# Attention scores from high and low halves, and the keys' token mix moved to the receptance stage

## The chip, the cores and the metric

The kernel runs on one core of a Trainium2 chip. The metric is the device time in microseconds; three runs of the kernel before took 915.26, 916.33 and 917.14 us, so the median is 916.33 us. A difference under about 0.2% (1.8 us) can't be told from none here.

## The reference, cut to what matters

Four batches, 12 heads, 448 tokens, head size 64. Sigmoid attention feeds a two-layer gated mix over tokens and channels, and that feeds a mixer; only the parts that this case touches are shown in full.

```python
scores = scale * np.matmul(q, k.transpose(0, 1, 3, 2)) - np.log(S)
attn = 1.0 / (1.0 + np.exp(-scores))
x = np.matmul(attn, v)                      # heads side by side: (4, 448, 768)
xk = mu_k * x + (1.0 - mu_k) * x_prev       # x_prev: x one token later
xr = mu_r * x + (1.0 - mu_r) * x_prev
r = 1.0 / (1.0 + np.exp(-(xr @ w_r)))       # receptance
x = r * (np.maximum(xk @ w_k, 0.0) ** 2 @ w_v)
...                                         # mixer: w_tok1, w_tok2, w_ch1, w_ch2
```

## The kernel before, in words

The kernel works on two batches at a time, so everything happens twice. One round has three parts, written out one after the other in program order (the order on each engine is the order of the calls; nothing reorders it).

**Attention** takes 12 units. A unit is one batch and one pair of heads: the two heads lie in partitions 0 to 63 and 64 to 127 of a tile `heads[i % 3]`, which holds the keys, values and queries of that unit. `scores(i)` makes the scores in four chunks of 128 keys. For each chunk TensorE multiplies keys by queries, one matmul for each head, in plain float32, with 64 contraction rows each (L160); the two heads use the two row halves of the array. ScalarE turns a chunk into sigmoids (L169). `values(i)` multiplies the sigmoids by the values, again in float32, one head in each column half of the array (L176), and ScalarE copies the result to `xe` (L348), a tile of one pair of heads and both batches. After every second unit `mix` makes `xr` and `xk` of that pair on VectorE: four instructions each (L186 to L191), the last two of which split the mixed tile into a high half in float32r and the low remainder. Between these, in the first round only, ScalarE and VectorE prepare the first weights (`w_form` L195 and L196, `w_join` L199 and L202, `w_high` L240, `w_low` L244).

**First part**: six output tiles of receptance (`w_r` against `xr`), eight of `w_k` against `xk`, six of `w_v`, then the token mixer. Every product runs in `products` (L299) as three passes in float32r: high by high, high by low, low by high. Weights are prepared ahead of use in small steps that `tick` issues between products.

**Second part**: the channel mixer, whose last products also issue the loads of the next round's first two units.

SyncE issues all loads in one queue (`load_kq`, `load_v`, `w_raw`); a load waits there until its buffer is free.

Of the kernel before, what the change touches and what calls it, by code (L numbers as in the profile page):

```python
# [37 lines left out]
def kernel(  # L38
# [19 lines left out]
    def pool(name, bufs, **kw):  # L58
        return ctx.enter_context(tc.tile_pool(name=name, bufs=bufs, **kw))

    const = pool("const", 1)
    wraw, wpool, wsplit = pool("wraw", 3), pool("wpool", 3), pool("wsplit", 3)
    tmps = pool("tmps", 2)
    psum = pool("psum", 4, space=PSUM)

# [8 lines left out]
    two = const.tile([P, 2 * 4 * 2 * C], F32R, tag="two", name="two")  # L74
    three = const.tile([P, 4 * W], F32R, tag="three", name="three")
    rows = const.tile([P, NT, W], F32, tag="rows", name="rows")
    xes = [const.tile([P, 2, 1 + S], F32, tag="xe%d" % i, name="xe") for i in range(2)]

    def two_parts(t, kt):
        n = kt * W  # L80
# [17 lines left out]
    def beside(ap):  # L98
        return ap.rearrange("p (b n) -> p b n", b=2)

    heads = [const.tile([P, 2 * 4 * P + S], F32, tag="qkv%d" % i, name="qkv") for i in range(3)]
    kns = [t[:, : 4 * P] for t in heads]
    vns = [t[:, 4 * P : 8 * P].rearrange("p (h c d) -> p h c d", h=2, c=4) for t in heads]
    qns = [t[:, 8 * P :] for t in heads]

    def new_ps():
        return psum.tile([P, 1024], F32, tag="ps", name="ps")
# [12 lines left out]
    def load_v(i):  # L120
        b, pr = units[i]
        SP.dma_start(out=vns[i % 3], in_=v[b * NPAIR + pr])
# [29 lines left out]
    turn = [0]  # L152
    att = {}

    def scores(i):
        for c in range(4):
            ps = new_ps()
            for h in range(2):
                me = slice(h * D, h * D + D)
                PE.matmul(  # L160
                    ps[:, h * 512 : h * 512 + S],
                    kns[i % 3][me, c * P : (c + 1) * P],
                    qns[i % 3][me],
                    start=True,
                    stop=True,
                )
            a = beside(rows[:, turn[0] % NT])
            turn[0] += 1
            ACT.activation(a, banks(ps), AF.Sigmoid, bias=-math.log(S), scale=1.0 / math.sqrt(D))  # L169
            att[c] = a  # L170
# [10 lines left out]
    def mix(name, t, x, xe):  # L181
        m, om = mus[name]
        hi, lo = (p[:, t] for p in x)
        mixed = tmps.tile([P, W], F32, tag="tmp", name="mix")
        dst = beside(mixed)
        DVE.tensor_scalar(out=dst, in0=xe[:, :, 0:S], scalar1=om[:, t : t + 1], scalar2=None, op0=ALU.mult)  # L186
        DVE.scalar_tensor_tensor(
            out=dst, in0=xe[:, :, 1:], scalar=m[:, t : t + 1], in1=dst, op0=ALU.mult, op1=ALU.add
        )
        DVE.tensor_copy(hi, mixed)  # L190
        DVE.tensor_tensor(out=lo, in0=mixed, in1=f32(hi), op=ALU.subtract)  # L191
# [134 lines left out]
    def attention(b0):  # L326
        base = b0 * NPAIR
        for i in range(base, base + 2 * NPAIR):
            p, t, xe = i - base, (i - base) // 2, xes[(i - base) // 2 % 2]
            if i + 2 < base + 2 * NPAIR:  # L330
                load_kq(i + 2)
                if p:
                    load_v(i + 2)
            scores(i)
            if b0 == 0:
                if p < 3:
                    w_raw(p + 1)
                if p in (2, 4, 6, 8):
                    w_form(p // 2)
                    w_join(p // 2)  # L340
                if p in (3, 5, 7):
                    w_high((p - 1) // 2)
                    w_low((p - 1) // 2)
                    w_raw((p - 1) // 2 + 3)
            ps = values(i, xe)
            if p == 0 and i + 2 < base + 2 * NPAIR:
                load_v(i + 2)
            ACT.copy(xe[:, p % 2, 1:], ps[:, :S])  # L348
            if p % 2:
                mix("r", t, xr, xe)  # L350
                mix("k", t, xk, xe)

    def first_part(b0):
        if b0 == 0:
            tok2_load()
        for m in range(NT):
            w = weights()
            ps = new_ps()
            products(ps, WIDE, against(w, xr, NT))
            ACT.activation(rows[:, m], ps[:, :W], AF.Sigmoid)  # L360
            if b0 == 0 and m < 3:
                tok2_stage(m)

        for m in range(F // P):
            w = weights()
            ps = new_ps()
            products(ps, WIDE, against(w, xk, NT))
            hi, lo = kk(m)
            t = tmps.tile([P, W], F32, tag="tmp", name="sq")
            ACT.activation(t, ps[:, :W], AF.Relu)  # L370
            DVE.tensor_tensor(out=t, in0=t, in1=t, op=ALU.mult)
            ACT.copy(hi, t)
            DVE.tensor_tensor(out=lo, in0=t, in1=f32(hi), op=ALU.subtract)

        for m in range(NT):
            ps = new_ps()
            for part in range(2):
                w = weights()
                parts = [(w[0][:, t], w[1][:, t], *kk(4 * part + t)) for t in range(4)]
                hooks = {2: lambda: y_transpose(m - 1)} if m and part == 0 else {}  # L380
                products(ps, WIDE, parts, 4 * part, 8, hooks)
            DVE.tensor_tensor(out=rows[:, m], in0=rows[:, m], in1=ps[:, :W], op=ALU.mult)  # L382

        wt1 = [weights()]
        held = due[:]
        due.clear()
        for f in held:
            f()
        i = use[0]
        use[0] += 1  # L390
        wt1.append(halves.pop(i))
        for piece in range(3):
            ps = new_ps()
            ms = slice(2 * piece, 2 * piece + 2)
            for j in range(2):
                wh, wl = wt1[j]
                x = [t[:, :, ms].rearrange("p r m b c -> p r (m b c)") for t in y]
                parts = [(wh[:, r], wl[:, r], x[0][:, r], x[1][:, r] if r < 3 else None) for r in range(4)]
                products(ps[:, j * 512 : (j + 1) * 512], ((0, 512),), parts)
                if piece == 0 and j == 0:  # L400
                    y_transpose(NT - 1)
            hi, lo = (t[:, :, ms].rearrange("p j m b c -> p j (m b c)") for t in h1)
            psv = ps.rearrange("p (j n) -> p j n", j=2)
            ACT.activation(hi, psv, AF.Relu)
            DVE.scalar_tensor_tensor(out=lo, in0=psv, scalar=0.0, in1=f32(hi), op0=ALU.max, op1=ALU.subtract)
        due[:] = ahead(i)

        for m in range(NT):
            ps = new_ps()
            for b in range(2):  # L410
                parts = [(h1[0][:, j, m, b], h1[1][:, j, m, b], wt2h[:, j], wt2l[:, j]) for j in range(2)]
                products(ps[:, b * 512 : b * 512 + S], ((0, S),), parts)
            hi, lo = (beside(p[:, m]) for p in u)
            r = beside(rows[:, m])
            DVE.tensor_tensor(out=r, in0=r, in1=banks(ps), op=ALU.add)  # L415
            ACT.copy(hi, r)  # L416
            DVE.tensor_tensor(out=lo, in0=r, in1=f32(hi), op=ALU.subtract)  # L417

    def second_part(b0):
        for half in range(2):  # L420
            for f in range(6):
                w = weights()
                ps = new_ps()
                products(ps, WIDE, against(w, u, NT))
                hi, lo = (p[:, f] for p in h2)
                ACT.activation(hi, ps[:, :W], AF.Relu)  # L426
                DVE.scalar_tensor_tensor(  # L427
                    out=lo, in0=ps[:, :W], scalar=0.0, in1=f32(hi), op0=ALU.max, op1=ALU.subtract
                )
            for m in range(NT):  # L430
                w = weights()
                ps = new_ps()
                products(ps, WIDE, against(w, h2, 6))
                DVE.tensor_tensor(out=rows[:, m], in0=rows[:, m], in1=ps[:, :W], op=ALU.add)  # L434
                if half:
                    for b in range(2):
                        SP.dma_start(
                            out=out[b0 + b, m * P : (m + 1) * P], in_=rows[:, m, b * S : (b + 1) * S]
                        )
                    if m == 3 and b0 + 2 < B:  # L440
                        for i in range(2):
                            load_kq((b0 + 2) * NPAIR + i)
                            load_v((b0 + 2) * NPAIR + i)

    for b0 in range(0, B, 2):
        attention(b0)
# [4 lines left out]
def lay_out(x):  # L451
# [3 lines left out]
    def chunks(w, parts=1):  # L455
# [9 lines left out]
    tail = v[:, :, 3 * P :].transpose(0, 2, 1, 3)[:, :, :, None]  # L465
    y = {
        "q": qt,
        "k": np.concatenate([kt, kt[:, :, 3 * P :]], axis=2),
        "v": np.concatenate([head, np.concatenate([tail, np.zeros_like(tail)], axis=1)], axis=3),
        "moe_mu_k": x["moe_mu_k"].reshape(NT, P).T,  # L470
        "moe_mu_r": x["moe_mu_r"].reshape(NT, P).T,
        "moe_w_k": chunks(x["moe_w_k"]),
# [51 lines left out]
```

## Time and profile before

| | us |
|---|---|
| median of the runs | 916.33 |
| profiled execution, whole | 914.43 |
| its span on the core | 912.7 |
| TensorE busy | 900.8 (99%) |
| VectorE busy | 505.3 (55%) |
| ScalarE busy | 420.0 (46%) |
| scores, matmuls L160, busy | 78.9 |
| values, matmuls L176, busy | 77.4 |

The span is one execution from its first to its last instruction on the core; the 1.7 us between it and the execution's own time lie around it. TensorE is busy nearly all the time, so a share of time tells little: what counts is how long each stretch of matmuls takes. The two attention stretches run from 5.85 to 82.22 us and from 457.0 to 533.4 us. A matmul's duration in the profile reaches from its start to its modelled end, and several are in the array at once; the distance from one start to the next tells what one costs.

### The profile page before, as it was taken

The numbers are of one execution on the slowest core, as the hardware profiler recorded it, in microseconds if no ns is written. First come the engines' busy times: TensorE is split into PE (matmuls) and PEld (weight loads), VectorE is DVE, ScalarE is ACT, GpSimd is POOL, SyncE is SP. The second block draws the span as 40 slices with busy tenths as digits, with TensorE's granted clock in tenths as the row PEclk, the third lists the DMA queues.
The fourth block names the chain that finished last, engine by engine and source line by source line (L and its number), as shares of the span: only waits on it lengthen the run. The fifth ranks groups of instructions, "written<-read, shape, count | busy, mean of one in ns | idle before, by whom it ended". The sixth has DMA issues, their size and how long they took to land.

```text
span 912.7 us, 10954 instructions
## 1 busy us (share of the span) xinstructions
PE 900.8 (99%) x4464; PEld 723.8 (79%) x4464; DVE 505.3 (55%) x563; ACT 420.0 (46%) x550; POOL 1.2 (0%) x9
## 2 busy tenths in 40 slices
PE   9999999999999999999999999999999999999997
PEld 3335888888887888888843468888988878888886
DVE  1776546656657555555535564465566575555551
ACT  5784645544434443343355644455444354334420
POOL 0000000000000000000000000000000000000000
PEclk9999999999999999999999999999999999999999
DMA  7542232223321333334654213222224123333311
GB/s 268 184 155 75 97 112 81 70 89 97 131 100 35 122 121 104 104 104 149 244 170 121 78 35 119 93 90 81 93 93 150 58 70 104 127 116 104 104 61 60
DMA packets 29426, 99.67 MB, mean 109 GB/s; under 512 B 3520, under 2 KB 9664, under 8 KB 29376
## 3 DMA queue, kind: packets, MB, share of 16 engines
q1 hardware_dynamic: 29376, 98.98, 32.7%
q8 instruction: 35, 0.57, 0.3%
q14 instruction: 15, 0.12, 0.0%
HBM read 93.46 MB, written 5.51 MB: 108 GB/s over the span
## 4 chain that ended last, share of the span: by engine, by line
PE 92%; DVE 5%; ACT 2%; issue 0%; POOL 0%; ACTq 0%; POOLq 0%
PE ps L299 74%; PE ps L160 8%; PE ps L176 8%; DVE two L417 1%; DVE rows L415 1%; ACT two L416 1%; PE ps L319 1%; DVE wd L199 1%; DVE wd L202 1%; PE ps L132 1%; ACT wd L195 0%; ACT raw L196 0%; DVE rows L382 0%; DVE two L322 0%; ACT whi L240 0%
## 5 line engine op out<-in xcount | busy, mean ns | idle before, releaser
L299 PE MATMUL ps<-one,whi 128*128 128x512 f32 (+1 forms) x1152 | 280.7, 365 | 0.0
L299 PE MATMUL ps<-two,whi 128*128 128x512 f32 (+1 forms) x1044 | 261.8, 367 | 4.1 <-ACT two L416 2.3
L299 PEld LDWEIGHTS ps<-one,whi 128*128 128x128 f32 x1152 | 208.1, 188 | 25.0 <-PE ps L176 0.7
L299 PEld LDWEIGHTS ps<-two,whi 128*128 128x128 f32 x1044 | 189.0, 188 | 30.3 <-ACT two L416 3.8
L299 PE MATMUL ps<-one,wlo 128*128 128x512 f32 x576 | 163.1, 364 | 0.0
L299 PE MATMUL ps<-two,wlo 128*128 128x512 f32 (+1 forms) x528 | 154.8, 367 | 0.0
L240 ACT CAST whi<-wd 128x768 fp32r<-128x768 f32 (+1 forms) x104 | 80.6, 775 | 138.4 <-PE ps L299 91.7
L244 DVE TENSOR_TENSOR wlo<-wd,whi 128x768 fp32r<-128x768 f32 (+1 forms) x104 | 91.6, 881 | 41.6 <-ACT whi L240 41.6
L299 PEld LDWEIGHTS ps<-one,wlo 128*128 128x128 f32 x576 | 104.4, 188 | 12.0
L199 DVE SCALAR_TENSOR_TENSOR wd<-wd,raw 128x768 uint32<-128x768 uint32 (+1 forms) x104 | 92.3, 887 | 30.5 <-ACT raw L196 27.9
L299 PEld LDWEIGHTS ps<-two,wlo 128*128 128x128 f32 x528 | 96.0, 188 | 12.2
L202 DVE SCALAR_TENSOR_TENSOR wd<-raw,wd 128x768 uint32<-128x768 uint32 (+1 forms) x104 | 92.2, 887 | 3.6
L169 ACT ACTIVATE rows<-ps 128x896 f32<-128x896 f32 x96 | 80.3, 924 | 21.5 <-PE ps L160 21.5
L195 ACT ACTIVATE wd<-raw 128x768 f32<-128x768 f32 (+1 forms) x104 | 88.1, 847 | 0.0
L196 ACT ACTIVATE raw<-raw 128x768 uint32<-128x768 uint32 (+1 forms) x104 | 86.6, 833 | 0.0
L160 PE MATMUL ps<-qkv 64*128 64x448 f32 x384 | 78.9, 550 | 0.0
L176 PE MATMUL ps<-rows,qkv 128*64 128x448 f32 x384 | 77.4, 545 | 0.0
L434 DVE TENSOR_TENSOR rows<-rows,ps 128x896 f32<-128x896 f32 x24 | 26.1, 1088 | 81.0 <-PE ps L299 81.0
L160 PEld LDWEIGHTS ps<-qkv 64*128 64x128 f32 x384 | 35.3, 188 | 42.8 <-issue 38.0
L176 PEld LDWEIGHTS ps<-rows,qkv 128*64 128x64 f32 x384 | 25.4, 136 | 49.1 <-issue 32.5
L426 ACT ACTIVATE one<-ps 128x896 fp32r<-128x896 f32 x24 | 22.0, 918 | 88.6 <-PE ps L299 88.6
L427 DVE SCALAR_TENSOR_TENSOR one<-ps,one 128x896 fp32r<-128x896 f32 x24 | 26.2, 1091 | 65.8 <-ACT one L426 65.8
(57 smaller groups left out, 443.6 us busy)
## 6 DMA issues: line engine op xcount, KB each, us to landing
raw<-in_moe_w_ch_dram SPq DMA_DIRECT2D x48, 768.0 KB, 4.1
raw<-in_moe_w_k_dram SPq DMA_DIRECT2D x16, 768.0 KB, 4.2
raw<-in_moe_w_v_dram SPq DMA_DIRECT2D x24, 512.0 KB, 3.6
raw<-in_moe_w_r_dram SPq DMA_DIRECT2D x12, 768.0 KB, 4.3
qkv<-in_k_dram SPq DMA_DIRECT2D x24, 256.0 KB, 2.8
qkv<-in_v_dram SPq DMA_DIRECT2D x24, 256.0 KB, 2.7
qkv<-in_q_dram SPq DMA_DIRECT2D x24, 224.0 KB, 3.0
out_dram<-rows SPq DMA_DIRECT2D x24, 224.0 KB, 2.2
```

The lines of the kernel that those rows point to most:

```text
L160: PE.matmul(ps[:, h * 512 : h * 512 + S], kns[i % 3][me, c * P : (c + 1) * P], qns[i % 3][me], start=True, stop=True,)
L169: ACT.activation(a, banks(ps), AF.Sigmoid, bias=-math.log(S), scale=1.0 / math.sqrt(D))
L176: PE.matmul(ps[h * D : h * D + D, :S], vns[i % 3][:, h, c], att[c][:, h], start=(c == 0), stop=(c == 3))
L195: ACT.activation(f32(dst), f32(raw[..., 1]), AF.Copy, scale=2.0**-112)
L196: ACT.activation(raw[..., 0], raw[..., 0], AF.Copy, bias=0.4375, scale=0.875 * 2.0**-29)
L199: DVE.scalar_tensor_tensor(out=dst, in0=dst, scalar=3, in1=raw[..., 0], op0=ALU.logical_shift_left, op1=ALU.bitwise_or)
L202: DVE.scalar_tensor_tensor(out=dst, in0=raw[..., 1], scalar=0x80000000, in1=dst, op0=ALU.bitwise_and, op1=ALU.bitwise_or)
L240: ACT.copy(halves[i][0], forms[i])
L244: DVE.tensor_tensor(out=halves[i][1], in0=forms.pop(i), in1=f32(halves[i][0]), op=ALU.subtract)
L299: PE.matmul(ps[:, a : a + cols], w, x[:, a : a + cols], start=(i == 0 and n == 0), stop=(i == count - 1 and n == len(passes) - 1),)
L427: DVE.scalar_tensor_tensor(out=lo, in0=ps[:, :W], scalar=0.0, in1=f32(hi), op0=ALU.max, op1=ALU.subtract)
L434: DVE.tensor_tensor(out=rows[:, m], in0=rows[:, m], in1=ps[:, :W], op=ALU.add)
```

## The change

- `scores(i)` takes the keys and queries of every unit but the first (`i == 0`) as a high half and a low half, both in float32r, and makes three passes: high by high, high by low, low by high. Each pass has one matmul for each head, so a chunk has six matmul calls instead of two.
- A new function `split_kq(i)` makes the halves on VectorE, in two instructions over the keys and queries side by side: a cast and a subtraction. It is called for unit `i + 1` right behind `scores(i)`, and for the first unit of the second round in the last products of the second part. The halves lie in the tile `three`, in two sets that alternate.
- `mix("k", ...)` leaves attention; it now stands behind each of the six receptance products. So `xe` has six tiles instead of two.
- The last key chunk takes the last 128 of 448 keys, so keys are loaded without the 64 repeated columns; the values' padding changes with it. The pool of weight forms has two buffers instead of three.

```diff
-    wraw, wpool, wsplit = pool("wraw", 3), pool("wpool", 3), pool("wsplit", 3)
+    wraw, wpool, wsplit = pool("wraw", 3), pool("wpool", 2), pool("wsplit", 3)
...
-    xes = [const.tile([P, 2, 1 + S], F32, tag="xe%d" % i, name="xe") for i in range(2)]
+    xes = [const.tile([P, 2, 1 + S], F32, tag="xe%d" % i, name="xe") for i in range(NT)]
...
+    kq_high = [three[:, i * 4 * S : i * 4 * S + 2 * S] for i in range(2)]
+    kq_low = [three[:, i * 4 * S + 2 * S : (i + 1) * 4 * S] for i in range(2)]
...
+    def split_kq(i):
+        hi, lo, x = kq_high[i % 2], kq_low[i % 2], heads[i % 3][:, : 2 * S]
+        DVE.tensor_copy(hi, x)
+        DVE.tensor_tensor(out=lo, in0=x, in1=f32(hi), op=ALU.subtract)
+
     def scores(i):
+        hi, lo = kq_high[i % 2], kq_low[i % 2]
         for c in range(4):
             ps = new_ps()
-            for h in range(2):
-                me = slice(h * D, h * D + D)
-                PE.matmul(
-                    ps[:, h * 512 : h * 512 + S],
-                    kns[i % 3][me, c * P : (c + 1) * P],
-                    qns[i % 3][me],
-                    start=True,
-                    stop=True,
-                )
+            cs = slice(c * P, (c + 1) * P) if c < 3 else slice(S - P, S)
+            if i == 0:
+                passes = [(kns[0], qns[0])]
+            else:
+                passes = [(x[:, :S], y[:, S:]) for x, y in ((hi, hi), (hi, lo), (lo, hi))]
+            for n, (x, y) in enumerate(passes):
+                for h in range(2):
+                    me = slice(h * D, h * D + D)
+                    PE.matmul(
+                        ps[:, h * 512 : h * 512 + S],
+                        x[me, cs],
+                        y[me],
+                        start=(n == 0),
+                        stop=(n == len(passes) - 1),
+                    )
...
             scores(i)
+            if i + 1 < base + 2 * NPAIR:
+                split_kq(i + 1)
...
                 mix("r", t, xr, xe)
-                mix("k", t, xk, xe)
...
             ACT.activation(rows[:, m], ps[:, :W], AF.Sigmoid)
+            mix("k", m, xk, xes[m])
...
+                    if m == 4 and b0 + 2 < B:
+                        split_kq((b0 + 2) * NPAIR)
```

On TensorE, the scores of the second unit, at the start of attention, stand in the kernel before as eight matmuls on the loaded tile `qkv`, each call one row here (the first six; `ps` are the accumulators, one for each chunk):

```order
L160 MATMUL ps_158<-qkv_82 128x448 [waits DMAHW4_49,DMAHW3_49,PE_49]
L160 MATMUL ps_158<-qkv_82 128x448
L160 MATMUL ps_162<-qkv_82 128x448 [waits PE_49]
L160 MATMUL ps_162<-qkv_82 128x448
L160 MATMUL ps_166<-qkv_82 128x448 [waits PE_49]
L160 MATMUL ps_166<-qkv_82 128x448
```

In the changed kernel the same scores are four groups of six on the tile `three`:

```order
L174 MATMUL ps_168<-three_77 128x448 [waits DVE_49,PE_49]
L174 MATMUL ps_168<-three_77 128x448
L174 MATMUL ps_168<-three_77 128x448 [waits DVE_49]
L174 MATMUL ps_168<-three_77 128x448 x3
L174 MATMUL ps_176<-three_77 128x448 [waits PE_49]
L174 MATMUL ps_176<-three_77 128x448 x5
L174 MATMUL ps_184<-three_77 128x448 [waits PE_49]
L174 MATMUL ps_184<-three_77 128x448 x5
L174 MATMUL ps_192<-three_77 128x448 [waits Activation_49]
L174 MATMUL ps_192<-three_77 128x448 x5
```

Where the first matmul waited for two loads it now waits for VectorE (the cast), and the first of the second pass waits for VectorE once more (the subtraction).

On VectorE, in the middle of the first round's attention, after the copy of an odd unit's values, the kernel before has both mixes (`omr` and `omk` are one minus the two mixing weights, `mur` and `muk` the weights, `one` and `two` the tiles of `xr` and `xk`) and then the weight forms:

```order
L186 TENSOR_SCALAR mix<-xe,omr 128x896 [waits Activation_49]
L187 SCALAR_TENSOR_TENSOR mix<-xe,mur,mix 128x896 [waits DVE_49]
L190 CAST one<-mix 128x896 [waits DVE_49]
L191 TENSOR_TENSOR one<-mix,one 128x896 [waits DVE_49]
L186 TENSOR_SCALAR mix<-xe,omk 128x896
L187 SCALAR_TENSOR_TENSOR mix<-xe,muk,mix 128x896 [waits DVE_49]
L190 CAST two<-mix 128x896 [waits DVE_49]
L191 TENSOR_TENSOR two<-mix,two 128x896 [waits DVE_49]
L199 SCALAR_TENSOR_TENSOR wd<-wd,raw 128x768 [waits DMAHW7_49,Activation_49]
L202 SCALAR_TENSOR_TENSOR wd<-raw,wd 128x768 [waits DVE_49]
```

The changed kernel has at that place:

```order
L200 TENSOR_SCALAR mix<-xe,omr 128x896 [waits Activation_49,Pool_49]
L201 SCALAR_TENSOR_TENSOR mix<-xe,mur,mix 128x896 [waits DVE_49]
L204 CAST one<-mix 128x896 [waits DVE_49]
L205 TENSOR_TENSOR one<-mix,one 128x896 [waits DVE_49]
L159 CAST three<-qkv 128x896 [waits DMAHW3_49,DMAHW2_49,PE_49]
L160 TENSOR_TENSOR three<-qkv,three 128x896 [waits DVE_49]
L213 SCALAR_TENSOR_TENSOR wd<-wd,raw 128x768 [waits Activation_49]
L216 SCALAR_TENSOR_TENSOR wd<-raw,wd 128x768 [waits DVE_49]
L159 CAST three<-qkv 128x896 [waits DMAHW7_49,DMAHW6_49,PE_49]
L160 TENSOR_TENSOR three<-qkv,three 128x896 [waits DVE_49]
```

The four instructions of the keys' mix are gone, and two splits stand there: one behind the mix, for the next unit, and one behind the weight forms, for the unit after it.

## Rows read from the trace of the kernel before

**Rows 1.** The page: engines (busy us, share, count), and the chain that ended last, by line.
```profile
PE 900.8 (99%) x4464; PEld 723.8 (79%) x4464; DVE 505.3 (55%) x563; ACT 420.0 (46%) x550; POOL 1.2 (0%) x9
PE ps L299 74%; PE ps L160 8%; PE ps L176 8%; DVE two L417 1%; DVE rows L415 1%; ACT two L416 1%; PE ps L319 1%; DVE wd L199 1%; DVE wd L202 1%; PE ps L132 1%; ACT wd L195 0%; ACT raw L196 0%; DVE rows L382 0%; DVE two L322 0%; ACT whi L240 0%
```

**Rows 2.** Busy time by stretch: both attentions, the first receptance stage.
```profile
core 0: us, PE busy (x) PEld busy (x) DVE busy (x) ACT busy (x) POOL busy (x), PEclk, DMA share, GB/s
5.85:82.22 76.37, 76.37 (x385) 30.46 (x384) 45.68 (x53) 54.71 (x70) 0.00 (x0) 1.00 0.50 165
82.40:126.00 43.60, 43.60 (x218) 39.06 (x216) 24.90 (x29) 19.64 (x27) 0.00 (x0) 1.00 0.33 114
457.00:533.40 76.40, 76.40 (x386) 30.30 (x385) 36.21 (x41) 46.02 (x59) 0.00 (x0) 1.00 0.35 107
```

**Rows 3.** Timeline, one unit of attention on TensorE (start us, us).
```profile
31.51 3.28 PE L160 MATMUL ps<-qkv 64*128 64x448 f32 x16
34.72 3.23 PE L176 MATMUL ps<-rows,qkv 128*64 128x448 f32 x16
37.88 1.40 PE L160 MATMUL ps<-qkv 64*128 64x448 f32 x6
```

**Rows 4.** Timeline, the weight loads of the same scores.
```profile
31.51 0.30 PEld L160 LDWEIGHTS ps<-qkv 64*128 64x128 f32 x4 [0.70 <-issue]
31.99 0.19 PEld L160 LDWEIGHTS ps<-qkv 64*128 64x128 f32 x2 [0.18 <-issue]
...
33.87 0.19 PEld L160 LDWEIGHTS ps<-qkv 64*128 64x128 f32 x2 [0.18 <-issue]
```

**Rows 5.** Groups by line and shape: names, count | busy us, mean ns | idle us.
```profile
L160 PE MATMUL ps<-qkv 64*128 64x448 f32 x384 | 78.9, 550 | 0.0
L299 PE MATMUL ps<-wt2h,one 128*128 128x448 f32 x96 | 27.7, 365 | 0.0
L160 PEld LDWEIGHTS ps<-qkv 64*128 64x128 f32 x384 | 35.3, 188 | 42.8 <-issue 38.0 <-PE ps L160 4.2 <-ACT rows L169 0.4
```

**Rows 6.** Timeline, TensorE, float32r products of 448 columns in the token mixer.
```profile
268.96 0.37 PE L299 MATMUL ps<-wt2l,one 128*128 128x448 f32 x1
...
278.16 0.37 PE L299 MATMUL ps<-wt2l,one 128*128 128x448 f32 x1
```

**Rows 7.** Timeline, VectorE in that unit of attention.
```profile
32.27 0.69 DVE L186 TENSOR_SCALAR mix<-xe,omr 128x896 f32<-128x896 f32 x1 [0.94 <-ACT xe L348]
...
34.17 0.63 DVE L190 CAST one<-mix 128x896 fp32r<-128x896 f32 x1
34.84 1.09 DVE L191 TENSOR_TENSOR one<-mix,one 128x896 fp32r<-128x896 f32 x1
35.85 0.68 DVE L186 TENSOR_SCALAR mix<-xe,omk 128x896 f32<-128x896 f32 x1
```

**Rows 8.** Timeline, ScalarE in that unit of attention.
```profile
31.63 0.53 ACT L348 COPY xe<-ps 128x448 f32<-128x448 f32 x1 [1.30 <-PE ps L176]
32.64 3.35 ACT L169 ACTIVATE rows<-ps 128x896 f32<-128x896 f32 x4 [0.48 <-PE ps L160]
35.84 0.96 ACT L195 ACTIVATE wd<-raw 128x768 f32<-128x768 f32 x1
36.68 0.96 ACT L196 ACTIVATE raw<-raw 128x768 uint32<-128x768 uint32 x1
```

**Rows 9.** Timeline, VectorE in the second receptance product.
```profile
92.01 0.63 DVE L199 SCALAR_TENSOR_TENSOR rows<-rows 128x448 uint32<-128x448 uint32 x1 [1.66 <-ACT rows L196]
92.68 0.62 DVE L202 SCALAR_TENSOR_TENSOR rows<-rows 128x448 uint32<-128x448 uint32 x1
93.22 0.95 DVE L244 TENSOR_TENSOR wlo<-wd,whi 128x768 fp32r<-128x768 f32 x1
...
95.33 0.96 DVE L202 SCALAR_TENSOR_TENSOR wd<-raw,wd 128x768 uint32<-128x768 uint32 x1
99.20 0.63 DVE L199 SCALAR_TENSOR_TENSOR rows<-rows 128x448 uint32<-128x448 uint32 x1 [2.92 <-ACT rows L196]
```

More of the change, by code (lines that the diff above doesn't have):

```diff
@@ L99, in beside @@
         return ap.rearrange("p (b n) -> p b n", b=2)
[L101 to L104, printed above, removed]
+    heads = [const.tile([P, 2 * S + 4 * P], F32, tag="qkv%d" % i, name="qkv") for i in range(3)]
+    kns = [t[:, :S] for t in heads]
+    qns = [t[:, S : 2 * S] for t in heads]
+    vns = [t[:, 2 * S :].rearrange("p (h c d) -> p h c d", h=2, c=4) for t in heads]
+    kq_high = [three[:, i * 4 * S : i * 4 * S + 2 * S] for i in range(2)]
+    kq_low = [three[:, i * 4 * S + 2 * S : (i + 1) * 4 * S] for i in range(2)]
     def new_ps():
@@ L328, in attention @@
         for i in range(base, base + 2 * NPAIR):
-            p, t, xe = i - base, (i - base) // 2, xes[(i - base) // 2 % 2]
+            p, t, xe = i - base, (i - base) // 2, xes[(i - base) // 2]
             if i + 2 < base + 2 * NPAIR:
@@ L467, in lay_out @@
         "q": qt,
-        "k": np.concatenate([kt, kt[:, :, 3 * P :]], axis=2),
-        "v": np.concatenate([head, np.concatenate([tail, np.zeros_like(tail)], axis=1)], axis=3),
+        "k": kt,
+        "v": np.concatenate([head, np.concatenate([np.zeros_like(tail), tail], axis=1)], axis=3),
         "moe_mu_k": x["moe_mu_k"].reshape(NT, P).T,
```

## The prediction

> **What bounds the kernel now.** I read the engines of the page first and the chain that ended last beside them [rows 1]: TensorE is busy 99% of the span, and the chain runs 74% through the products, 8% through the scores and 8% through the values. So a change is worth what it takes from or adds to TensorE's own stretches. Next come the stretches [rows 2]: in both attentions TensorE is busy all of 76.4 us at a granted clock of 1.00, 2.4 GHz, while VectorE is busy 45.7 us in the first and 36.2 us in the second, ScalarE 54.7 and 46.0 us. Twelve units share 76.37 us, 6.36 us each. The timeline of one unit splits this [rows 3]: scores from 31.51 to 34.72 us, 3.21 us; values from there to 37.88 us, 3.16 us. The row counts 16 matmuls for the eight calls of the scores, two for each float32 call.
>
> How do these 16 come to 3.21 us? Their weight loads show it [rows 4]: after the first four, two loads begin together every 0.376 us (from 31.99 to 33.87 us five steps, 1.88 us). Eight such steps make 3.01 us; the remaining 0.20 us is the start and end of the stretch, about half of it at the start, where the second pair comes 0.48 us after the first instead of 0.376. One step holds two matmuls of 0.55 us each, as the group's mean tells [rows 5], so the two lie in the array at the same time. A float32r matmul of the same 448 columns lasts 0.365 us [rows 5]: the float32 record is 0.185 us longer, which is the 187 ns that 448 columns take at 2.4 GHz. A float32 record thus holds the columns twice, a chunk of two heads costs two steps, 0.75 us, and the heads do overlap.
>
> **The scores, part by part.** A chunk now has three passes with two float32r matmuls each. If these overlap as the float32 ones do, a pass costs one float32r step. No row shows float32r in row halves. The nearest is float32r over the whole array with 448 columns: 45 of them from 268.96 to 278.16 us, 9.20 us, 0.204 us each [rows 6] (the 15 groups between hold three each). I take 0.204, since it has the same type, the same columns and a weight load before each matmul. The low end is half of a float32 step, 0.188. The high end is two matmuls in turn, 0.409.
>
> With 0.204 a unit's scores cost 12 x 0.204 + 0.20 = 2.65 us instead of 3.21, and the unit 5.81 us instead of 6.36: 0.55 us less. The first unit keeps float32, so 23 units gain 12.7 us.
>
> The Trainium skill has a rule against this, in "TensorE: Matmul & The Clock Gate", Part 3: it says that a weight load overlaps running matmuls only where the row groups differ. In this trace the loads of both heads run in the middle of a stretch whose matmuls fill both row halves without a gap [rows 3, 4], so the trace does not agree; by the rule each pass would wait for its own load, and the time would be that of the third rival below. The same part says that matmuls in different row groups run together, 3.07 times as fast for four tiles, which agrees with the two overlapping heads; by this half of the page the sum stays as it is.
>
> **The splits.** A split is two VectorE instructions of the shape and types that the mix's last two have: 0.67 us from the cast's start to the next, then 1.09 us [rows 7]. In attention a split for each unit (1.76 us) replaces the keys' mix for every second (35.85 - 32.27 = 3.58 us for the like mix of `xr`): VectorE's work stays the same. What matters is when a split is done, since TensorE now waits for it. The tight place is an even unit, where the split for the next unit stands behind the mix. Counted from the scores' start at 31.51 us: the mix ends its turn at 35.85, +4.34; the high halves are there at about +5.0 and the low halves at 4.34 + 0.67 + 1.09 + 0.11 = +6.21 (0.11 us for the signal, as between the copy's end on ScalarE at 32.16 us and the mix on VectorE [rows 7, 8]). TensorE would start the next scores at +5.81 and needs the low halves with the second pass, 0.30 us later (the start's 0.10 and one pass), at +6.11. So it waits some 0.10 us in ten such units, five in each round: 1.0 us together. Behind that waiting matmul stands all the rest of TensorE's work, and ScalarE's first sigmoid waits for it. Other units have time: their split comes behind the weight forms, at about +9.8 against +11.6 where it is needed.
>
> ScalarE: four sigmoids 3.35 us, a copy 0.53, and in the first round's even units two narrowings of 1.8 together [rows 8]: 5.7 us in a unit of 5.81, and well under it in the odd ones. The first sigmoid starts 1.13 us after the scores do; it will start about 0.15 us sooner, with the shorter first chunk, and the last ends near +4.3, while the values need it at 2.65 + 2.3 = +4.95. This holds, with 0.6 us to spare. Were that cover gone, the excess would come on top of ten or so units.
>
> **The keys' mix in the receptance stage.** It is 3.58 us for each of six products of 7.27 us (43.60 us for six, [rows 2]). The busiest are those in which the token mixer's second weights are prepared: 1.25 us of VectorE for those and 2.9 us for the weights [rows 9], with the mix 7.7 us, 0.45 us too many in each of three. The backlog of 1.3 us is worked off in the other three, which hold 6.5 us. Nobody waits for it: low halves are needed a product later, the last keys' mix only by the sixth row block of the first `w_k` product, some 6 us into it, and it is done about 3 us before. What the mix takes first is the 2.92 us in which VectorE now idles between a product's weight forms and the next instruction [rows 9]. I cost it at nothing; without cover it is at most that 1.3 us a round.
>
> **The rest** is nothing: the split for the second round stands in a product with 3 us of idle VectorE (the mixes take 3.58 in a like one); loads of keys are 32 KB smaller and, with scores off the loaded tile, wait on SyncE for a split that ends before the scores that they waited for; a weight form is used up before the form two later is begun, so two buffers do.
>
> **The sum.** -12.7 + 1.0 = -11.7 us. The profiled execution takes 914.43 us (912.7 span and 1.7 around it), so it would take 902.7. The median is 1.9 us above that execution, 916.33: predicted 904.6. With 0.188 a unit would be 5.62 us (0.74 less, 17.0 us gained), but the low halves at +6.21 then hold ten units up by 0.30 us: 14.0 us in all, 902.3.
>
> **Rivals.**
> - *VectorE becomes the bound in attention.* For it: the tight units have nothing to spare. If a mix or a split takes 0.4 us longer, beside the faster matmuls, or a pass costs a little more than over the whole array, 10 to 23 units lose 0.2 to 0.4 us: 2 to 7 us are given back, and the time is 907 to 911. Against it: VectorE's durations are the same to 0.01 us wherever the rows stand.
> - *The two heads' float32r matmuls run in turn.* For it: no row shows that type in row halves. Against it: the float32 matmuls overlap at the same places [rows 4, 5]. Price: 12 x 0.409 + 0.20 + 3.16 = 8.27 us for a unit, 1.91 more, 23 times: 44 us slower, 960. It decides from the point where a pass of both heads costs (6.36 - 3.36) / 12 = 0.25 us; above that the change loses.
> - *Loads are not hidden.* A pass then costs 0.204 plus a load of 0.188 [rows 5], 0.392: a unit 8.06 us, 39 us slower, 955. Against it: loads are hidden now [rows 4], though a step has 0.376 us for them and would have 0.204.
> - *No change.* The gain could be used up by all of the first rival together; for that the passes would have to cost 0.25, between the two regimes, for which no row speaks.
>
> **Chances.** Forecast (901 to 907 us) 0.70; VectorE bound or slower passes (907 to 912) 0.15; no change 0.03; in turn 0.08; loads not hidden 0.04. Faster by over 0.2% (1.8 us, about what a measurement of this kernel tells from none) 0.85, within it 0.03, slower 0.12. The range, 900.5 to 911, holds the forecast, both ends that a pass in parallel allows and most of the first rival; about 0.2 stays out, nearly all of it the two slow cases.
>
> **What would show it.** In the profile after: twelve steps of 0.20 us in a unit's scores, with two matmuls beginning within some 10 ns of each other (steps of 0.4 or single starts: in turn, or loads not hidden); attention stretches of 70 to 71 us instead of 76.4; in every second unit a wait of TensorE for VectorE's subtraction of about 0.1 us (more, with a gap in TensorE's busy time: the first rival); the receptance stage still 43.6 us, with VectorE busy some 21 us more there than now and no wait of TensorE (if it is longer, the mix is not hidden). The forecast is wrong if attention stays over 73 us, or if a stretch outside attention grows by over 1 us.

## The result, and the profile after

The changed kernel takes 907.16 us (905.45 to 908.29, five runs), the kernel before 916.33 us beside it (five runs): a ratio of 0.9899, with a 95% interval of 0.9882 to 0.9916. It is 9.2 us faster; 11.7 were forecast, 904.6 us, and the time lies in the range of 900.5 to 911.

The page of the changed kernel has the same picture as [rows 1], with VectorE busier by 36.5 us (engines, and the chain that ended last by line):

```profile
PE 892.1 (99%) x4648; PEld 742.5 (82%) x4648; DVE 541.8 (60%) x609; ACT 420.0 (46%) x550; POOL 1.3 (0%) x13
PE ps L313 75%; PE ps L190 8%; PE ps L174 7%; DVE two L433 1%; DVE rows L431 1%; ACT two L432 1%; PE ps L333 1%; DVE wd L213 1%; DVE wd L216 1%; PE ps L134 0%; ACT wd L209 0%; ACT raw L210 0%; DVE rows L398 0%; DVE two L336 0%; ACT whi L254 0%
```

The gain is where it was looked for. Busy time by stretch, attention and receptance of both rounds (columns as in [rows 2]):

```profile
5.30:76.11 70.81, 70.81 (x474) 38.12 (x473) 46.29 (x55) 54.51 (x70) 0.00 (x0) 1.00 0.55 179
76.11:119.70 43.59, 43.59 (x215) 38.99 (x216) 39.54 (x47) 19.73 (x27) 0.00 (x0) 1.00 0.34 112
452.58:522.46 69.88, 69.88 (x482) 39.10 (x481) 36.89 (x43) 46.05 (x59) 0.00 (x0) 1.00 0.39 120
522.46:566.00 43.54, 43.54 (x214) 38.98 (x215) 39.14 (x44) 19.13 (x24) 0.00 (x0) 1.00 0.29 93
```

Attention takes 70.81 and 69.88 us. The stretch that [rows 2] gives for the first attention of the kernel before is a little short: by the chain that ended last (the profile's list of what held up what, in order of time) it runs from 5.92 to 82.50 us, 76.58 us, and the second from 457.03 to 533.41 us, 76.38 us. So attention is 12.3 us shorter. Of this 0.2 us isn't the change's: the first unit's scores, which stay in float32, took 3.41 us in the one profile and 3.21 in the other. Ahead of them the matmuls that only warm TensorE up took 4.66 and 4.05 us. The kernel before,

```profile
1.26 4.66 PE ps L132 x12
5.92 3.41 PE ps L160 x16
```

and the changed one:

```profile
1.26 4.05 PE ps L134 x12
5.30 3.21 PE ps L174 x16
```

Both differ from execution to execution: in a second profile of the changed kernel they took 4.66 and 3.50 us. So 12.1 us are the change's, and 0.8 us at the start are chance.

VectorE's work in attention stayed the same (46.3 and 36.9 us, before 45.7 and 36.2). In the receptance stage VectorE is busy 39.5 us instead of 24.9, and TensorE still has no gap in it. The lengths of these stretches were chosen and don't tell how long the stage is; the first matmul of the next products, on `xk`, does. On the timelines of the kernel before, of the changed one, and of the one with the split ahead and padding (among the experiments; its keys' mix is in the same place), that matmul is

```profile
126.17 0.97 PE L299 MATMUL ps<-two,whi 128*128 128x512 f32 x4
```
```profile
120.07 0.98 PE L313 MATMUL ps<-two,whi 128*128 128x512 f32 x4
```
```profile
119.47 0.97 PE L314 MATMUL ps<-two,whi 128*128 128x512 f32 x4
```

The stage's first matmul starts at 82.43, 76.04 and 75.72 us, so the stage lasts 43.74, 44.03 and 43.75 us. The 0.29 us are the products' longer step, which comes below; the mix itself adds nothing.

One unit on TensorE, by the timeline, answers to [rows 3]: the scores' 24 matmuls stand from 29.10 to 31.73 us, 2.63 us instead of 3.21; the values still take 3.16 us.

```profile
29.10 2.70 PE L174 MATMUL ps<-three 64*128 64x448 f32 x24
31.73 3.23 PE L190 MATMUL ps<-rows,qkv 128*64 128x448 f32 x16
34.89 1.22 PE L174 MATMUL ps<-three 64*128 64x448 f32 x8
```

Without the 0.20 us of start and end, twelve passes share 2.43 us: 0.203 us each. The group's mean is 0.374 us for one matmul, longer than a step, so the records of successive passes overlap; and since two matmuls share a step, the two heads run beside each other, as the float32 ones did:

```profile
L174 PE MATMUL ps<-three 64*128 64x448 f32 x552 | 63.3, 374 | 0.0
```

The tight place is there too. VectorE behind the mix of an odd unit (answers to [rows 7]), and TensorE's weight loads at the same time:

```profile
33.44 0.62 DVE L159 CAST three<-qkv 128x896 fp32r<-128x896 f32 x1
34.09 1.09 DVE L160 TENSOR_TENSOR three<-qkv,three 128x896 fp32r<-128x896 f32 x1
```
```profile
34.89 0.18 PEld L174 LDWEIGHTS ps<-three 64*128 64x128 f32 x2 [0.70 <-issue]
35.23 1.31 PEld L174 LDWEIGHTS ps<-three 64*128 64x128 f32 x14 [0.16 <-DVE three L160]
```

The subtraction ends at 35.18 us, the second pass's weights start at 35.23, 0.34 us behind the first pass instead of 0.20 us behind. So the wait is 0.14 us here.

What the forecast did not have stands outside attention. The two longest pieces of the chain in each round, of the kernel before:

```profile
82.50 115.34 PE ps L299 x570
288.69 168.33 PE ps L299 x832
533.41 115.34 PE ps L299 x570
739.54 168.35 PE ps L299 x832
```

and of the changed kernel:

```profile
76.11 116.11 PE ps L313 x570
283.14 169.44 PE ps L313 x832
522.46 116.10 PE ps L313 x570
729.46 169.45 PE ps L313 x832
```

These products (`w_r`, `w_k` and the beginning of `w_v`; the channel mixer) have the same matmuls in both kernels, and take 0.7% longer: 3.7 us in all. What lies between the pieces is 0.2 us longer. With the 12.1 us gained in attention and the 0.8 us at the start this makes the 9.0 us by which the spans differ (912.7 and 903.7 us). The experiments ask first where the 3.7 us come from.

### The profile page after: what moved, and what is told of

Its sections match the earlier page's. It is cut to its first block, busy times and chain, and to the rows that moved or that the text cites. A ratio compares the mean times of both kernels' runs of the same rounds, so it can differ in the third digit from the quotient of the medians.

```text
span 903.7 us, 11370 instructions
## 1 busy us (share of the span) xinstructions
PE 892.1 (99%) x4648; PEld 742.5 (82%) x4648; DVE 541.8 (60%) x609; ACT 420.0 (46%) x550; POOL 1.3 (0%) x13
## 4 chain that ended last, share of the span: by engine, by line
PE 92%; DVE 5%; ACT 2%; issue 0%; POOL 0%; ACTq 0%; POOLq 0%
PE ps L313 75%; PE ps L190 8%; PE ps L174 7%; DVE two L433 1%; DVE rows L431 1%; ACT two L432 1%; PE ps L333 1%; DVE wd L213 1%; DVE wd L216 1%; PE ps L134 0%; ACT wd L209 0%; ACT raw L210 0%; DVE rows L398 0%; DVE two L336 0%; ACT whi L254 0%
## 5 line engine op out<-in xcount | busy, mean ns | idle before, releaser
L313 PEld LDWEIGHTS ps<-one,wlo 128*128 128x128 f32 x576 | 104.8, 188 | 12.3
L174 PEld LDWEIGHTS ps<-three 64*128 64x128 f32 x552 | 50.3, 184 | 20.1 <-issue 15.8
L174 PE MATMUL ps<-three 64*128 64x448 f32 x552 | 63.3, 374 | 0.0
```

What stands on the lines that cost most here:

```text
L174: PE.matmul(ps[:, h * 512 : h * 512 + S], x[me, cs], y[me], start=(n == 0), stop=(n == len(passes) - 1),)
L313: PE.matmul(ps[:, a : a + cols], w, x[:, a : a + cols], start=(i == 0 and n == 0), stop=(i == count - 1 and n == len(passes) - 1),)
```

## The experiments

The kernel before ran beside each of three groups of experiments. Its median was 915.00 us beside the same kernels again, the move alone and the split ahead of the mix; 916.61 beside the paddings to 96 and 480, the mix that stays and the heads one after the other; 915.14 beside the rest. A ratio is to that median, so ratios compare better than times do.

**The same two kernels again.** No edit.

> The kernel before, unchanged, profiled once more, because the products outside attention took 0.6% longer in the profile of the changed kernel (115.3 to 116.1 us in the first long stretch, 168.3 to 169.4 in the second). Theory L (the layout of the tiles in memory sets the step): the mean distance of a 512- and a 384-column product stays 404 ns, the two stretches 115.3 and 168.3 us. Theory E (the execution sets it, by chance): it may come out anywhere between 398 and 407 ns, the stretches up to 116.1 and 169.4 us.

> The changed kernel, unchanged, profiled once more. Theory L: 407 ns for the pair of products again, stretches of 116.1 and 169.4 us. Theory E: another figure is as likely, down to 404 ns and 115.3 and 168.3 us. Both: the scores' steps are 0.20 us and attention takes 70.8 and 69.9 us, as in the first profile.

The kernel before took 916.47 us this time, the changed one 907.50. The chain's pieces of the kernel before:

```profile
82.48 115.33 PE ps L299 x570
288.42 168.33 PE ps L299 x832
533.13 116.10 PE ps L299 x570
739.99 169.91 PE ps L299 x832
```

and of the changed one:

```profile
77.05 116.11 PE ps L313 x570
284.11 170.47 PE ps L313 x832
524.45 116.09 PE ps L313 x570
731.47 169.45 PE ps L313 x832
```

The kernel before shows both figures, one in each round; the changed kernel shows the long one four times out of four. The granted clock is 1.00 in the piece of 116.10 us too. Neither theory is out: the kernel before can run at either step, the changed one perhaps only at the slow one. (169.91 and 170.47 hold a fall of the clock as well, see the last section; so do 169.79, 171.00 and 170.85 below.)

**The move of the mix alone.**

```diff
-            if i == 0:
-                passes = [(kns[0], qns[0])]
+            if True:
+                passes = [(kns[i % 3], qns[i % 3])]
...
-            if i + 1 < base + 2 * NPAIR:
-                split_kq(i + 1)
...
-                    if m == 4 and b0 + 2 < B:
-                        split_kq((b0 + 2) * NPAIR)
```

> Only the keys' mix moved to the receptance stage; scores stay in float32 and there are no splits; the tiles lie as in the changed kernel. Theory (the mix is hidden at both places): 916 us, within 1.5 us of the kernel before; attention 76.4 us, the receptance stage 43.6 us with no wait of TensorE. Rival (the move itself is worth something): over 2 us off 916 in either direction. Theory L would add 3 to 4 us in the products (407 ns for a pair), theory E nothing in the median.

919.87 us, 1.0059 times the kernel before (1.0046 to 1.0073): slower. The second attention lasts from 460.11 to 536.49 us, 76.38 us as before, and the receptance stage is no longer than in the changed kernel (44.03 us), so the mix is hidden at both places. The first long pieces are at 116.10 us in both rounds. The move brings no time of its own, and something that comes with it costs 4 to 5 us, where theory L had 3 to 4; in the profile 1.4 us of it is a fall of the clock (one second long piece takes 170.87 us, the other 169.46).

**Padding ahead of the weights.** The order on the engines is not touched: one unused tile in front of the token mixer's second weights moves these, the raw and formed weights, the halves and the temporary tiles, which lie behind it. `one`, `two` and `three`, which the products multiply with the halves, lie ahead of it, at the same bytes in every kernel here. In the kernel before the halves begin at byte 96 of a block of 1024, in the changed one at 480. The one is put at the other's place (the first edit is on the kernel of the next experiment, with the split ahead of the mix):

```diff
+    const.tile([P, 160], F32, tag="pad", name="pad")
     wt2h = const.tile([P, 2, S], F32R, tag="wt2h", name="wt2h")
```
```diff
+    const.tile([P, 96], F32, tag="pad", name="pad")
     wt2h = const.tile([P, 2, S], F32R, tag="wt2h", name="wt2h")
```

> The kernel with the split ahead of the mix, and 640 unused bytes in each partition ahead of the weight tiles, so that the high and low weights begin at the same place in a block of 1024 bytes as in the kernel before (96 instead of 480). Theory L (where the weights lie sets the products' step): 404 ns for a pair of products, stretches of 115.3 and 168.3 us, 3.5 us faster than without the padding, 902. Theory E (chance, or something else in the program): 407 ns, 116.1 and 169.4 us, 905.5.

> The kernel before with 384 unused bytes in each partition ahead of the weight tiles, which puts the weights where the changed kernel has them in a block of 1024 bytes (480 instead of 96). Theory L: 407 ns for a pair of products, stretches of 116.1 and 169.4 us, 3.5 us slower than before, 919. Theory E: as the kernel before, 915 to 916, with stretches of 115.3 and 168.3 us in most executions.

With padding the changed kernel (split ahead) takes 902.64 us, 0.9843 times the kernel before (0.9825 to 0.9861); without it 905.47, 0.9895 times. The padded kernel before takes 919.19 us, 1.0027 times the unpadded one (1.0014 to 1.0039). The pieces, of the first:

```profile
75.80 115.34 PE ps L314 x570
281.79 169.79 PE ps L314 x832
521.26 115.34 PE ps L314 x570
727.26 168.35 PE ps L314 x832
```

and of the padded kernel before:

```profile
82.51 116.10 PE ps L300 x570
289.54 171.00 PE ps L300 x832
536.92 116.10 PE ps L300 x570
743.96 170.85 PE ps L300 x832
```

Bytes that nobody reads move the first piece from 116.1 to 115.3 us in one kernel and from 115.3 to 116.1 in the other. Theory L holds, but for the one round of the unchanged kernel at 116.10, and two more places say a little about what counts:

```diff
-    const.tile([P, 160], F32, tag="pad", name="pad")
+    const.tile([P, 136], F32, tag="pad", name="pad")
```
```diff
-    const.tile([P, 160], F32, tag="pad", name="pad")
+    const.tile([P, 32], F32, tag="pad", name="pad")
```

> The kernel with the split ahead of the mix and 544 unused bytes ahead of the weight tiles: high and low weights begin at 0 in a block of 1024 bytes. Theory L1 (what counts is the place within 64 bytes: 32 at both places tried so far, so this one is new): a third figure for the pair of products. Theory L2 (what counts is the place within 1024 bytes): any of 404 to 407 ns. Theory L3 (96 is special by chance, others are at 407): 905.5. A gain below 902 would be a better place.

> The same with 128 unused bytes: the weights begin at 608 in a block of 1024 bytes, which is 96 in a block of 512 or 256 bytes. If the place within 512 bytes or less counts: 404 ns, 115.3 and 168.3 us, 902. If the place within 1024 counts: 407 ns and 905.5.

At 0 the kernel takes 909.62 us and the piece 117.04 us, a third figure; at 608 it takes 902.39 us (0.9860, 0.9847 to 0.9874) and 115.34 us. Over all profiles of this study, the first long piece of each round:

| weights begin, in 1024 bytes | rounds seen | first long piece, us |
|---|---|---|
| 96 | 6 | 115.3 five times, 116.1 once |
| 608 | 2 | 115.3 |
| 480 | 18 | 116.1 each time |
| 0 | 2 | 117.0 |

96 and 608 are the same place in 512 or 256 bytes, 480 and 0 are others. In 128 or 64 bytes 96 and 480 would be the same, and they differ. So the four places fit a rule by the place within 512 or 256 bytes, for the tiles behind the padding; four places don't prove it. Which of these tiles it is was not tried; the halves are the ones that TensorE reads in these products. Why the step follows the place stays open, and so does the one round of the kernel before at 116.1.

**The split ahead of the mix.**

```diff
                 split_kq(i + 1)
+            if p and p % 2 == 0:
+                mix("r", t - 1, xr, xes[t - 1])
...
-            if p % 2:
+            if p == 2 * NPAIR - 1:
                 mix("r", t, xr, xe)
```

> The changed kernel with the mix of an odd unit issued one unit later, behind the split instead of ahead of it, so that no scores wait for a split. Theory (the ten waits of about 0.1 us are what the splits cost): attention 70.1 and 69.5 us instead of 70.8 and 69.9, 1.1 us faster than the changed kernel, 906. Rival (VectorE's queue only shifts the wait, to the weights or to the first receptance product): no gain or a loss of 1 us.

905.47 us (0.9895, 0.9882 to 0.9909): by the ratio it can't be told from the changed kernel (0.9899), and what it gains is read from the profile. The second attention takes 69.65 us (452.84 to 522.49) instead of 69.88, and no scores wait for VectorE; odd units' scores fall from 2.77 and 2.71 us to 2.63 to 2.67. In the first round 0.35 us are gained although the first scores, which have nothing to do with the edit, took 3.49 us instead of 3.21. So the waits were worth about 0.9 us, near the prediction's 1.0, and nothing else came late.

**The mix stays in attention.**

```diff
                 mix("r", t, xr, xe)
+                mix("k", t, xk, xe)
...
-            mix("k", m, xk, xes[m])
```

> Only the scores' three passes and the splits; the keys' mix stays in attention, behind the mix of the receptance. Theory (VectorE's queue decides when the split is there, so the move of the mix is what makes the passes pay): in ten even units the split comes 3.6 us later, the scores behind it wait some 3.7 us, attention takes some 18 us more in each round, 943 us in all, slower than the kernel before. Rival (the split is early enough wherever it stands): 907 us as the changed kernel.

954.26 us, 1.0411 times the kernel before (1.0389 to 1.0433): without the move, the three passes lose. TensorE's waits (total us, times, longest):

```profile
PE ps L174 <- DVE three L159: 27.8, 10, 2.8
PE ps L174 <- DVE three L160: 5.6, 10, 0.6
```

Ten waits of 3.3 us each, where 3.7 were expected: 33 of the 47 us that it takes more than the changed kernel. For the rest the profile shows one cause, the clock: it is no longer granted in full in attention, as the third value from the end of two stretches shows (PEclk 0.91 from 44.0 us on, 0.89 in the second round),

```profile
44.00:99.90 55.90, 45.77 (x279) 25.96 (x277) 37.97 (x44) 31.79 (x40) 0.00 (x0) 0.91 0.27 82
509.80:570.30 60.50, 48.04 (x281) 27.58 (x281) 33.73 (x40) 27.78 (x34) 0.00 (x0) 0.89 0.17 53
```

and the values behind a long wait take 3.69 us on the timeline (at 30.44 us) instead of 3.23. Behind eight of the ten waits the clock falls (to between 0.50 and 0.68 over a stretch of 3 us). An estimate of what this costs is the missing share of the clock times the length: 0.09 of 55.9 us, 0.11 of 60.5 and, from 26.0 to 44.0 us, 0.09 of 18.0, together 13 of the 14 us. I had not priced that.

**Heads one after the other in the program.**

```diff
-            for n, (x, y) in enumerate(passes):
-                for h in range(2):
+            for h in range(2):
+                for n, (x, y) in enumerate(passes):
```

> The changed kernel with the order of the scores' matmuls turned: all three passes of the first head, then all three of the second, the same six matmuls in a chunk. Theory (the two heads run together only where their matmuls follow each other): matmuls overlap only at the borders, a chunk costs four steps of 0.20 us instead of three, 0.8 us more for a unit, 19 us for 23 units, 926. If even the borders don't overlap, six steps: 56 us, 963. Rival (the heads overlap whatever the order, since the engine looks ahead): 907.

908.68 us (0.9910, 0.9889 to 0.9931): the theory fell. The matmuls of a chunk are issued three of one head, then three of the other, and the chain still has

```profile
18.63 2.64 PE ps L174 x24
21.27 3.16 PE ps L190 x16
24.43 2.97 PE ps L174 x24
```

the 2.64 us of even units; odd units have 2.97 instead of 2.77, since now the second matmul already waits for the low halves. Neighbourhood in the program isn't what makes the heads overlap. Nor does the compiler interleave them: the instruction stream that it makes of this kernel has three matmuls of the one row half, then three of the other. In the trace they begin in pairs all the same (at 18.56 and 18.57 us, then at 18.87 and 18.88), so TensorE lets the second head's first matmul begin ahead of two that stand before it. Where the low halves are late it doesn't pass the waiting matmul: in the unit of 2.97 us one matmul begins alone at 24.36 us and the next pair at 24.70. That half-filled step is the 0.2 us that odd units lose.

**Both heads in one row half.**

```diff
-                    me = slice(h * D, h * D + D)
+                    me = slice(0, D)
```

(in the scores alone; the second head's own scores are left out).

> The changed kernel with both heads' scores made from the first head's rows, so that all six matmuls of a chunk lie in one row half of the array (the second head's scores are then the first's: its own are left out). Theory (two matmuls run together only in different row halves; the engine looks ahead to find them, whatever the program order): a chunk costs six steps of 0.20 us, 2.4 us more for a unit, 56 us for 23 units, 963; that is the rival of the prediction in which the heads run in turn. Rival (any two matmuls of 64 rows run together): 907.

964.52 us, 1.0539 (1.0525 to 1.0553), as expected to 2 us. The timeline:

```profile
23.57 5.12 PE L174 MATMUL ps<-three 64*128 64x448 f32 x24
28.62 3.23 PE L190 MATMUL ps<-rows,qkv 128*64 128x448 f32 x16
```

The same 24 matmuls take 5.05 us to the next start instead of 2.63: (5.05 - 0.20) / 24 = 0.202 us, each by itself. So the overlap is the two row halves', and it is worth 57 us here, 3 of them in the first unit, whose float32 scores the edit changes too (6.35 instead of 3.21 us).

**Two passes.** The third pass is left out.

```diff
-                passes = [(x[:, :S], y[:, S:]) for x, y in ((hi, hi), (hi, lo), (lo, hi))]
+                passes = [(x[:, :S], y[:, S:]) for x, y in ((hi, hi), (hi, lo))]
```

> The changed kernel without the third pass of the scores (low keys by high queries is left out). Theory (VectorE's split bounds every second unit: the low halves are there 6.2 us after the scores of an even unit began, ScalarE's work fills 5.9 us of it in the first round): odd units lose 0.8 us, even units next to nothing beyond the waits that they have, 8 to 9 us in all, 898 to 899. Rival (only TensorE counts): 23 x 0.81 = 18.7 us, 888.

896.04 us, 0.9791 (0.9777 to 0.9804): 11.1 us less than the changed kernel (9.9 by the ratios), of the 18.7 that TensorE would save. In the profile attention takes 66.44 and 64.70 us, 9.6 less. The theory, with 8 to 9 us, is nearer, 1 to 2 us too low. The waits show VectorE's subtraction, ten times, as the bound that comes next:

```profile
PE ps L174 <- DVE three L160: 5.4, 10, 0.6
```

It isn't the only one: in the first round the chain ahead of two of these splits runs through a load of queries.

```profile
39.31 3.38 DMA qkv<-in_q_dram
50.31 3.37 DMA qkv<-in_q_dram
```

## Why the prediction was right, point by point

- *A pass of both heads costs one float32r step.* Right, and to size: 0.203 us against 0.204. The row it was taken from was the nearest in type and columns, although it had the whole array. That the two heads overlap by their row halves is shown by the kernel with both in one half; its 964.5 us are the rival in which they run in turn (960). That rival was about right in size and wrong in its condition: the type alone doesn't make the heads run in turn.
- *Weight loads are hidden.* Right: with no gap at 0.20 us a step, against the rule of the Trainium skill in "TensorE: Matmul & The Clock Gate", Part 3, that a load overlaps running matmuls only in other row groups. In the kernel with all matmuls in one row half loads had nowhere else to go, and a step was still 0.202 us. The same part's statement that matmuls keep program order does not agree with three steps for heads issued one after the other either: the compiled program had them in the order of the calls, and the trace has them begin in pairs. How TensorE does this stays open; the kernel's description above says that nothing reorders the calls, and that holds for the program alone.
- *Ten waits for the split, 1.0 us.* Right: 0.14 us in the first round and 0.08 in the second (odd units' scores 2.77 and 2.71 us against 2.63), 1.1 us in all; taking them away brought about 0.9. That the 0.14 us meets the forecast's 0.10 is in part luck: counted from the unit's start, the low halves came at +6.13 us instead of +6.21, and the second pass wanted them at +5.99 instead of +6.11, since it stands 0.20 us behind the first and not 0.30.
- *The keys' mix is hidden in the receptance stage.* Right: 43.75 us with the padding against 43.74 before, with VectorE busy 14.6 us more than before in the changed kernel's first such stage. The prediction had "some 21" there: the last pair's mix stood in this stage before the change already, and the last of the six ran on past the stage.
- *The rest is nothing.* This term was wrong. The six tiles of `xe` and the smaller tiles of keys, values and queries put the weights at another place, and the products outside attention took 3.7 us more, which the prediction costed at nothing. Padding takes that back. The prediction gave "a stretch outside attention grows by over 1 us" as a sign that it is wrong, and that sign came: the channel mixer's piece grew by 1.11 us in the first round and 1.10 in the second.
- *ScalarE holds.* Right: TensorE is busy throughout both attentions but for the waits above, and none of its waits there is for ScalarE.

In sum, in the two profiles: -12.1 in attention where -11.7 were forecast, +3.7 in the products and +0.2 between them that were not, and -0.8 at the start, which is chance. The time of 907.16 us, 2.6 us above the forecast, falls just among those that the prediction gave to VectorE as the bound or slower passes (907 to 912), but for another reason: attention lost no more to either than was forecast.

The kernel with the split ahead of the mix and padding beats both: 902.4 to 902.6 us, 0.984 to 0.986 of the kernel before.

## What to carry to other kernels

Price a new kind of matmul from the row that shares its type and columns, and look at whether the two halves of the array overlap, since that decides the sign. When work moves between engines, follow the queue that the new wait hangs on: here one moved mix was the difference between 9 us gained and 38 lost. And when tiles change size, look at the steps of the untouched matmuls: a third of the gain went there, and a few hundred unused bytes in each partition brought it back.

## What the runs showed of the hardware that was not expected

- The step of float32r products depends on where the weight tiles lie in the memory: 115.3, 116.1 or 117.0 us for the same 570 matmuls, with one round of 28 that the place doesn't explain.
- The clock falls in 8 of the 28 rounds at one place, where TensorE waits four times within 5 us, up to 0.9 us, for the mixer's halves. Stretches of the changed kernel in its second profile, and at the same place in its first (PEclk is the third value from the end):

```profile
282.90:287.00 4.10, 4.01 (x11) 3.06 (x12) 3.61 (x4) 3.31 (x5) 0.00 (x0) 0.58 0.00 0
```
```profile
282.00:286.00 4.00, 3.54 (x16) 2.86 (x17) 3.58 (x4) 3.18 (x4) 0.00 (x0) 1.00 0.00 0
```

  At 0.58 the clock was at 1.2 GHz for most of the stretch and at 2.4 for the rest, and the chain's piece behind its start took 170.47 instead of 169.44 us. Where runs of one kernel differ by about a microsecond this may be why: of the changed kernel's five runs the one with a mean clock of 0.999 took 905.45 us, the four with 0.997 took 907.10 to 908.29. That was not tried.
- With both heads in program order one after the other, three passes still took three steps (2.64 us for a unit): TensorE began a matmul of the other row half ahead of two that stood before it.
